# A sparse attention and mixture-of-experts kernel: half a batch more of loads requested ahead of each gate, with a longer FFN lag, a token in place of a drain, and a smaller, later gate

## The chip, the cores and the metric

The kernel runs on one core of one Trainium2 chip. The metric is the device time of one execution in microseconds (us). The engines are PE (matmul; PEld is its weight load), DVE (vector), ACT (scalar), POOL (which here, after some setup, only issues loads) and SP (which issues stores). Each run carries a label, fast or slow. For one core, slow only means over 1.5% above the fastest run of the same kernel.

## The reference, cut to what matters

```python
def _attn_ref(q, k, v):                       # B, H, S, D = 8, 8, 576, 64
    scores = (1 / np.sqrt(D)) * np.matmul(q, k.transpose(0, 1, 3, 2))
    # heads 0-3: the 32 newest positions; heads 4-7: every 4th of the 128 newest
    scores = np.where(masks[None], scores, -1e9)
    ...                                       # softmax
    return np.matmul(attn, v)

def _moe_ref(x, w_gate, w1, w2):              # x: (8, 576, 512); 8 experts, F = 1024
    logits = x.mean(axis=1) @ w_gate          # ONE expert for a whole batch row
    e_idx = np.argmax(logits, axis=1)
    ...                                       # gate_w: softmax weight of that expert
    out[b] = gate_w[b] * (np.maximum(x[b] @ w1[e], 0.0) @ w2[e])
```

Which expert's weights (2 MB of bf16 in SBUF) a batch needs is known only when its attention is finished. So these loads cannot be requested early. The loads of q, k and v could be.

Of the kernel before, what the change touches and what calls it, by code (L numbers as in the profile page):

```python
# [19 lines left out]
P = 128  # L20
B = 8
# [15 lines left out]
DLO = 1024  # L37
HALF = 288
NSLOT = 4
LAG = 6  # L40


@with_exitstack
def kernel(
# [9 lines left out]
):  # L54
    nc = tc.nc
    PSUM = bass.MemoryType.PSUM

    const = ctx.enter_context(tc.tile_pool(name="const", bufs=1))
    ldp = ctx.enter_context(tc.tile_pool(name="ld", bufs=4))
# [46 lines left out]

    GO = (1, 0)

    load_tiles(0)
    load_qk(0, GO[0])  # L110
    identb = const.tile([P, P], BF16, name="identb")
# [6 lines left out]
    nc.gpsimd.iota(dtt[:], pattern=[[1, 4], [4, 16]], base=0, channel_multiplier=-1)  # L118
    load_qk(0, GO[1])
    load_v(0, GO[1])  # L120
    load_tiles(1)
    load_qk(1, GO[0])
    load_v(1, GO[0])
    load_vt(1)
    load_qk(1, GO[1])
    load_v(1, GO[1])

    ones64 = const.tile([P, DH], BF16, name="ones64")
    nc.vector.memset(ones64[:], 1.0)
    wg_t = const.tile([P, 4, E], F32, name="wg_t")  # L130
    for a in range(2):
        for g in range(2):
# [112 lines left out]
    def av_work(b, n):  # L245
        s = state(b)
        g, h2 = GO[n // 2], n % 2
        nd = psN.tile([P, 3 * 512], F32, name="nd", tag="nd", space=PSUM)
        s["nd"] = nd
        vm, vt, pt = loads[b]["v", g], loads[b]["vt"], s["pt"][n]  # L250

        def mm(a, o, n, lhsT, rhs, start, view=None):
            oo = nd[half(a), o : o + n]
            if view is not None:
                oo = view(oo)
            nc.tensor.matmul(oo, lhsT=lhsT, rhs=rhs, start=start, stop=True, skip_group_check=True)  # L256

        def V(a, e, i):
            return vm[half(e), 2 * a + h2, i, :]
# [4 lines left out]
        def part_a():  # L264
# [28 lines left out]
            if g == 0:  # L293
                for a in range(2):
                    mm(a, DLO + 256, 64, ones64[half(0), :], pt[half(0), a, 4 * QB : NP], False)

        def part_b():
            nc.tensor.drain()
            for i in range(4):
                if g == 0:  # L300
                    for e in range(2):
                        for a in range(2):
                            o = NSO + 64 * i if e == 0 else NLO + 64 * (i + 1)
                            mm(a, o, 32, V(a, e, i), pt[half(e), a, QB * i + 64 : QB * i + 96], False)
                else:
                    for a in range(2):
                        mm(a, NLO + 80 * i, 32, V(a, 0, i), pt[half(0), a, QB * i + 64 : QB * i + 96], False)
            if g == 0:
                for e in range(2):
                    for a in range(2):  # L310
                        o = DSO if e == 0 else DLO + 64
                        mm(
                            a, o, 256, ones64[half(e), :], pc(a, e, 64, 96), False,
                            lambda x: x.rearrange("p (i n) -> p i n", n=64)[:, :, 0:32],
                        )
            else:
                for a in range(2):
                    tl = pt[half(0), a, 4 * QB : NP].rearrange("p (r m) -> p r m", r=4)
                    mm(
                        a, NLO, 320, vt[:, 4 * g + 2 * a + h2, :], tl, False,  # L320
                        lambda x: x.rearrange("p (r n) -> p r n", n=80)[:, :, 64:80],
                    )
                for a in range(2):
                    mm(
                        a, DLO, 320, ones64[half(0), :], pc(a, 0, 64, 96), False,
                        lambda x: x.rearrange("p (r n) -> p r n", n=80)[:, :, 0:32],
                    )
                for a in range(2):
                    tl = pt[half(0), a, 4 * QB : NP].rearrange("p (r m) -> p r m", r=4)
                    mm(  # L330
                        a, DLO, 320, ones64[half(0), :], tl, False,
                        lambda x: x.rearrange("p (r n) -> p r n", n=80)[:, :, 64:80],
                    )

        return part_a, part_b

    def emit_ln(b):
        s = st[b]
# [46 lines left out]
    def emit_gate(b):  # L385
        s = st[b]
        pooled = small.tile([P, 4], F32, name="pooled", tag="pooled")
        nc.vector.tensor_tensor(out=pooled[:], in0=s["pool"][:, 0, :], in1=s["pool"][:, 1, :], op=ALU.add)
        lgt = psM.tile([P, 512], F32, name="lgt", tag="M", space=PSUM)
        lg = lgt[:, 0:E]  # L390
        for c in range(4):
            nc.tensor.matmul(  # L392
                lg, lhsT=pooled[:, c : c + 1].to_broadcast([P, P]), rhs=wg_t[:, c, :], start=(c == 0), stop=(c == 3)
            )
        l_sb = small.tile([P, E], F32, name="l_sb", tag="l_sb")
        nc.vector.tensor_copy(out=l_sb[:], in_=lg)
        mx = small.tile([P, 8], F32, name="mx", tag="mx")
        mi = small.tile([P, 8], U32, name="mi", tag="mi")
        nc.vector.max_with_indices(mx[:], mi[:], l_sb[:])
        s["gate"] = (l_sb, mx)  # L400
        e_val = nc.values_load(mi[0:1, 0:1].bitcast(I32), engines=[ET.Pool], min_val=0, max_val=E - 1)
        w1b = wp.tile([P, 4, F], BF16, name="w1b", tag="w1b")
        w2b = wp.tile([P, 8, DM], BF16, name="w2b", tag="w2b")
        s["w1"], s["w2"] = w1b, w2b
        for a in range(2):
            for g in range(2):
                r0 = 256 * g + 128 * a
                nc.gpsimd.dma_start(  # L408
                    out=w1b[half(a), 2 * g : 2 * g + 2, :],
                    in_=moe_w1[ds(e_val, 1), r0 : r0 + 128, :].rearrange("e (h d) f -> d (e h) f", d=DH),  # L410
                )
        nb = b + 2
        if nb < B:
            load_tiles(nb)
            load_qk(nb, GO[0])
        nc.gpsimd.dma_start(out=w2b[:], in_=moe_w2[ds(e_val, 1)].rearrange("e (c p) f -> p (e c) f", p=P))
        if nb < B:
            load_v(nb, GO[0])
            load_vt(nb)
            load_qk(nb, GO[1])  # L420
            load_v(nb, GO[1])

    def emit_gate_w(b):
        s = st[b]
        l_sb, mx = s["gate"]
        negm = small.tile([P, 1], F32, name="negm", tag="negm")
        nc.vector.tensor_scalar_mul(out=negm[:], in0=mx[:, 0:1], scalar1=-1.0 / S)
        esum = small.tile([P, 1], F32, name="esum", tag="esum")
        etmp = small.tile([P, E], F32, name="etmp", tag="etmp")
        nc.scalar.activation(  # L430
            out=etmp[:], in_=l_sb[:], func=AF.Exp, scale=1.0 / S, bias=negm[:], accum_out=esum[:]
        )
        nc.vector.tensor_scalar_add(out=esum[:], in0=esum[:], scalar1=1e-9)
        gbc = small.tile([P, 1], F32, name="gbc", tag="gbc")
        nc.vector.reciprocal(out=gbc[:], in_=esum[:])  # L435
        s["gbc"] = gbc


    def ffn1(b, fc, hf, eng):
# [12 lines left out]
        else:  # L452
            nc.vector.tensor_scalar_max(out=o, in0=hm[:], scalar1=0.0)  # L453

    def ffn2(b, r, eng):
        s = st[b]
        om = psM.tile([P, DM], F32, name="om", tag="M", space=PSUM)
# [6 lines left out]
            nc.scalar.activation(out=osb[:], in_=om[:], func=AF.Copy, scale=s["gbc"][:])  # L464
        else:
            nc.vector.tensor_scalar_mul(out=osb[:], in0=om[:], scalar1=s["gbc"][:])  # L466
        nc.sync.dma_start(out=out[b, r * P : (r + 1) * P, :], in_=osb[:])

    def ffn_tail(b):
        s = st[b]  # L470
# [11 lines left out]
        osx = osp.tile([P, 256], F32, name="osx", tag="osx")  # L482
        nc.vector.tensor_scalar_mul(out=osx[:], in0=ox[:], scalar1=s["gbc"][:])
        for a in range(2):
            nc.sync.dma_start(out=out[b, 512:S, 256 * a : 256 * a + 256], in_=osx[half(a), :])


    ps0 = psS.tile([P, 2, 512], F32, name="psS", tag="S", space=PSUM)
# [11 lines left out]
    def run_T(t):  # L500
        for b, g, nm in tsched.get(t, []):
            emit_T(b, g, nm, 0, "D")
            emit_T(b, g, nm, 1, "A")

    run_T(-2)
    run_T(-1)
    for t in range(NA + LAG + 1):
        b, n = divmod(t, NSLOT)
        pb, pn = divmod(t - 1, NSLOT)
        fb, fk = divmod(t - LAG, NSLOT)  # L510
        att = t < NA
        prev = 0 <= t - 1 < NA
        run_T(t)
        if prev:
            pa, pbb = av_work(pb, pn)
            pa()
        if att:
            emit_S_mm(b, n)
            emit_exp(b, n)
        items = []  # L520
        if 0 <= fb < B:
            if fk < 2:
                for x in range(4):
                    items.append(lambda x=x: (ffn1(fb, 4 * fk + x, 0, "D"), ffn1(fb, 4 * fk + x, 1, "A")))
            elif fk == 2:
                items += [lambda: ffn2(fb, 0, "A"), lambda: ffn2(fb, 1, "D")]
            else:
                items += [lambda: ffn2(fb, 2, "A"), lambda: ffn2(fb, 3, "D"), lambda: ffn_tail(fb)]
        if prev:
            pbb()  # L530
            emit_ln(pb)
        if att:
            emit_mask(b, n)
        if prev:
            emit_rd(pb)
        k0 = len(items) // 2
        for f in items[:k0]:
            f()
        if prev:
            emit_norm(pb, pn)  # L540
        for f in items[k0:]:
            f()
        if prev and pn == NSLOT - 1:
            emit_gate(pb)
            emit_gate_w(pb)


# [28 lines left out]
```

## The kernel before: the parts that the change and the argument touch

Work is laid out in slots. Slot t runs scores (S), exp and mask for one quarter of a batch, and the product with v, the normalization and the division for the quarter of slot t-1. Batch b has slots 4b to 4b+3. Its k and q must be transposed on PE first: the first group of four heads (k in slot 4b-2, q in 4b-1), then the second group (k in slot 4b, q in 4b+1). The FFN of batch b is spread over four slots from slot 4b+LAG on: two of fc1 (`hm`, needs w1), two of fc2 (`om`, needs w2).

```python
LAG = 6
ldp = tc.tile_pool(name="ld", bufs=4)         # q, k, v: four batches
osp = tc.tile_pool(name="osp", bufs=3)        # output tiles
...
def part_b():                                 # second half of the product with v
    nc.tensor.drain()
    ...
def emit_gate(b):
    ...                                       # pooled sum; logits on 128 partitions
    e_val = nc.values_load(mi[0:1, 0:1].bitcast(I32), engines=[ET.Pool], ...)
    for a in range(2):
        for g in range(2):
            nc.gpsimd.dma_start(out=w1b[...], in_=moe_w1[ds(e_val, 1), ...])
    nb = b + 2
    if nb < B:
        load_tiles(nb)
        load_qk(nb, GO[0])                    # first group of batch b+2
    nc.gpsimd.dma_start(out=w2b[:], in_=moe_w2[ds(e_val, 1)]...)
    if nb < B:
        load_v(nb, GO[0]); load_vt(nb)
        load_qk(nb, GO[1]); load_v(nb, GO[1]) # second group of batch b+2
...
for t in range(NA + LAG + 1):
    run_T(t)                                  # transposes, first thing in a slot
    if prev: pa()                             # product, first half
    if att:  emit_S_mm(b, n); emit_exp(b, n)
    if prev: pbb(); emit_ln(pb)               # product, second half
    ...                                       # mask, half of the FFN, norm, other half
    if prev and pn == NSLOT - 1:
        emit_gate(pb); emit_gate_w(pb)        # gate of batch b: end of slot 4b+4
```

All loads go through POOL's one queue in program order.

The softmax here doesn't subtract the row's maximum and nothing guards it: scores larger than these inputs give would overflow.

## Time and profile before

| | before |
|---|---|
| time, median of 3 | 309.23 us (308.3 to 311.2) |
| PE / DVE / ACT busy | 72% / 43% / 42% |
| chain of waits | PE 44%, DMA 25% (k alone 20%) |
| mean granted PE clock | 0.895 |

No engine is full, so the chain of waits and the table of waits are the views to read. The waits table of the kernel before names who waited for whom; its columns are total us, how often, and the longest:

```profile
PEld L190 <- DMA km<-in_k_dram: 49.6, 8, 10.0
PE tp L190 <- DMA km<-in_k_dram: 47.9, 8, 9.8
...
PE hm L446 <- DMA w1b<-in_moe_w_dram: 11.7, 4, 6.5
...
PE lgt L392 <- DVE pooled L388: 9.7, 8, 2.7
```

PE waited 48 us in 8 pieces for k before a transpose. The same table, asked stretch by stretch, splits them: 8.7 us in two pieces at the start, 9.8 us behind gate 0, and 29.4 us in five steady batches (6.4, 8.0, 5.7, 5.9 and 3.4). The chain that ended last, in order of time (start, duration, what), shows the load of k once per batch; its pieces are about 9 us. Here is one batch of the kernel before:

```profile
144.93 9.13 DMA km<-in_k_dram
154.11 1.06 PE tp L190 x31
156.89 2.49 PE hm L446 x12
...
174.48 1.04 PE lgt L392 x8
179.84 9.14 DMA km<-in_k_dram
189.03 1.06 PE tp L190 x31
```

The gate's logits (174.48) come about 5 us before k is even requested (179.84), and k lands 9 us after that. The stretches of the kernel before give the length of each stretch, the busy us of PE, PEld, DVE, ACT and POOL (with counts) in it, then the granted clock, the DMA share and GB/s:

```profile
180.00:186.00 6.00, 3.13 (x26) 1.58 (x24) 1.91 (x6) 0.69 (x1) 4.46 (x7) 1.00 1.01 155
186.00:192.00 6.00, 2.85 (x90) 2.46 (x91) 0.76 (x1) 1.62 (x3) 2.12 (x3) 0.50 1.12 248
...
204.00:210.00 6.00, 4.93 (x46) 2.73 (x48) 2.29 (x7) 2.83 (x5) 0.00 (x0) 1.00 0.17 66
```

While PE stands (from 183 us), its granted clock falls to 0.50 and is still there when work resumes at 189 us. From 204 us, with the loads done, the DMA engines have little to do (share 0.17, 66 GB/s). That fall agrees with the Trainium skill, "TensorE: Matmul & The Clock Gate", Part 1, which says that a PE which has idled for a window is put on half clock until a busy window has passed.

### The profile page before, as it was taken

What the parts mean: (1) busy time and instruction counts of PE and PEld (TensorE: products, weight loads), DVE (VectorE), ACT (ScalarE), POOL (GpSimd) and SP (SyncE); (2) the same over time, 40 slices, a digit from 0 to 9 for tenths busy, and PEclk for the clock granted to TensorE, in tenths of its full rate; (3) what the DMA queues carried; (4) which work ended last, traced back from release to release, by engine and by line L of the source; (5) the groups of instructions that cost most, each with busy time, mean ns of one, the idle gap of its engine ahead of it and who ended that gap; (6) DMA issues with size and microseconds to landing.
All of it is one profiled execution on the core that took longest, in us unless ns stands there. A gap on an engine that the chain in (4) does not pass through costs nothing.

```text
span 309.2 us, 8991 instructions
## 1 busy us (share of the span) xinstructions
PE 223.7 (72%) x3936; PEld 151.6 (49%) x3936; DVE 131.7 (43%) x366; ACT 130.3 (42%) x225; POOL 80.7 (26%) x128
## 2 busy tenths in 40 slices
PE   1565508989299836999299865987599868981894
PEld 1554506754276514755177534754376535640652
DVE  3645413645155532654156532654255533430231
ACT  2465404654067403654057423654167441620230
POOL 8730272007310262005410083005510120021000
PEclk9999999997689985997879895997989996997699
DMA  7990099916997299914999189945999299029803
GB/s 101 185 177 4 9 169 203 127 71 91 217 206 81 79 180 227 173 38 100 193 215 117 72 131 238 198 56 104 195 220 111 72 174 182 2 75 213 140 36 119
DMA packets 49383, 40.97 MB, mean 133 GB/s; under 512 B 23744, under 2 KB 37056, under 8 KB 49344
## 3 DMA queue, kind: packets, MB, share of 16 engines
q0 software_dynamic: 42880, 30.94, 69.5%
q1 hardware_dynamic: 6464, 9.46, 8.9%
q8 instruction: 31, 0.51, 0.6%
q14 instruction: 8, 0.07, 0.1%
HBM read 61.88 MB, written 9.44 MB: 231 GB/s over the span
## 4 chain that ended last, share of the span: by engine, by line
PE 44%; DMA 25%; DVE 10%; issue 8%; ACT 6%; POOL 3%; POOLq 2%
DMA km<-in_k_dram 20%; PE hm L446 19%; PE om L459 10%; DMA w1b<-in_moe_w_dram 6%; PE nd L256 5%; PE tp L190 5%; DVE xt L373 3%; PE lgt L392 3%; ACT pt L233 3%; PE psS L209 3%; DVE ht L453 2%; DVE osb L466 2%; POOL w1b L408 2%; ACT qk L196 1%; DVE pt L240 1%
## 5 line engine op out<-in xcount | busy, mean ns | idle before, releaser
L446 PE MATMUL hm<-xt,w1b 128*128 128x288 bf16 x512 | 78.7, 314 | 12.4 <-DMA w1b<-in_moe_w_dram 11.7
L446 PEld LDWEIGHTS <-w1b 128*128 128x128 bf16 x512 | 53.3, 107 | 34.9 <-issue 11.2
L459 PE MATMUL om<-w2b,ht 128*128 128x512 bf16 x256 | 62.4, 401 | 0.0
L408 POOL DMA_DIRECT2D w1b<-in_moe_w_dram x32 | 19.1, 606 | 133.1 <-DVE gbc L435 61.8
L196 ACT ACTIVATE qk<-tp 128x576 bf16<-128x576 bf16 x32 | 23.2, 726 | 67.6 <-PE tp L190 67.6
L190 PE MATMUL tp<-ident,km 64*64 64x64 bf16 x576 | 16.3, 219 | 48.8 <-DMA km<-in_k_dram 47.9
L451 ACT ACTIVATE ht<-hm 128x288 bf16<-128x288 f32 x64 | 26.2, 409 | 50.3 <-PE hm L446 50.2
L198 DVE COPY qk<-tp 128x576 bf16<-128x576 bf16 x32 | 24.1, 756 | 45.4 <-PE tp L190 45.4
L453 DVE TENSOR_SCALAR ht<-hm 128x288 bf16<-128x288 f32 x64 | 29.2, 456 | 32.6 <-PE hm L446 31.9
L459 PEld LDWEIGHTS <-ht 128*128 128x128 bf16 x256 | 25.1, 103 | 31.1 <-issue 6.0
L190 PEld LDWEIGHTS <-km 64*64 64x64 bf16 x576 | 14.2, 133 | 52.0 <-DMA km<-in_k_dram 49.6
L373 DVE SCALAR_TENSOR_TENSOR xt<-nd,rd 128x320 bf16<-128x320 f32 x64 | 32.4, 544 | 13.9 <-ACT rd L346 13.9
L100 POOL DMA_DIRECT2D vm<-in_v_dram x32 | 23.9, 755 | 52.6 <-DMA w2b<-in_moe_w_dram 30.8
L240 DVE TENSOR_TENSOR pt<-pt,mk 128x896 bf16<-128x896 bf16 x32 | 20.0, 625 | 35.8 <-ACT pt L233 35.8
L233 ACT ACTIVATE pt<-psS 128x896 bf16<-128x896 f32 x32 | 29.1, 911 | 9.4 <-PE psS L209 8.5
L256 PE MATMUL nd<-pt,vm 64*64 64x64 bf16 (+2 forms) x896 | 25.2, 207 | 8.7 <-DVE xt L373 4.2
L256 PEld LDWEIGHTS <-vm 64*64 64x64 bf16 x896 | 18.2, 120 | 15.0 <-issue 14.0
L256 PE MATMUL nd<-pt,ones 64*64 64x128 bf16 (+3 forms) x288 | 24.1, 279 | 0.0
L346 ACT ACTIVATE rd<-lnd 128x576 f32<-128x576 f32 x32 | 21.8, 683 | 1.0
L466 DVE TENSOR_SCALAR osb<-om,gbc 128x512 f32<-128x512 f32 x16 | 12.0, 750 | 24.0 <-PE om L459 24.0
L340 ACT ACTIVATE lnd<-nd 128x576 f32<-128x576 f32 x32 | 20.8, 648 | 1.2 <-PE nd L256 1.2
L209 PE MATMUL psS<-qk 64*64 64x96 bf16 (+2 forms) x576 | 20.3, 247 | 0.0
(52 smaller groups left out, 183.5 us busy)
## 6 DMA issues: line engine op xcount, KB each, us to landing
w1b<-in_moe_w_dram POOLq DMA_DIRECT2D x32, 256.0 KB, 6.2
w2b<-in_moe_w_dram POOLq DMA_DIRECT2D x8, 1024.0 KB, 15.5
out_dram<-osb SPq DMA_DIRECT2D x32, 256.0 KB, 2.3
km<-in_k_dram POOLq DMA_DIRECT2D x16, 288.0 KB, 9.3
qm<-in_q_dram POOLq DMA_DIRECT2D x16, 288.0 KB, 10.8
vm<-in_v_dram POOLq DMA_DIRECT2D x8, 256.0 KB, 15.9
vm<-in_v_dram POOLq DMA_DIRECT2D x32, 64.0 KB, 11.3
out_dram<-osx SPq DMA_DIRECT2D x16, 64.0 KB, 7.7
```

The source lines that it names most:

```text
L190: nc.tensor.transpose(out=tp[half(a), j, :], in_=t[half(a), RH * jh + j, :], identity=ident2[half(a), :])
L196: nc.scalar.activation(out=o, in_=i, func=AF.Copy)
L198: nc.vector.tensor_copy(out=o, in_=i)
L209: nc.tensor.matmul(ps[half(e), a, o : o + rhs.free_size()], lhsT=lhsT, rhs=rhs, start=True, stop=True, skip_group_check=True)
L233: nc.scalar.activation(out=pt[:], in_=s["ps"][:, :, 0:NP], func=AF.Exp, scale=0.125)
L256: nc.tensor.matmul(oo, lhsT=lhsT, rhs=rhs, start=start, stop=True, skip_group_check=True)
L373: nc.vector.scalar_tensor_tensor(out=o, in0=a0, scalar=1.0, in1=a1, op0=ALU.mult, op1=ALU.mult, accum_out=s["pool"][:, w, c : c + 1],)
L408: nc.gpsimd.dma_start(out=w1b[half(a), 2 * g : 2 * g + 2, :], in_=moe_w1[ds(e_val, 1), r0 : r0 + 128, :].rearrange("e (h d) f -> d (e h) f ...
L446: nc.tensor.matmul(hm[:], lhsT=s["w1"][:, c, fc * P : (fc + 1) * P], rhs=s["xt"][:, c, cols], start=(c == 0), stop=(c == 3))
L451: nc.scalar.activation(out=o, in_=hm[:], func=AF.Relu)
L453: nc.vector.tensor_scalar_max(out=o, in0=hm[:], scalar1=0.0)
L459: nc.tensor.matmul(om[:], lhsT=s["ht"][:, fc, r * P : (r + 1) * P], rhs=s["w2"][:, fc, :], start=(fc == 0), stop=(fc == 7))
```

## The change

The intent: ask for half a batch more ahead of each gate; give the weights two more slots before the FFN wants them; take the PE drain, the wide logits and the wait for them out of PE's way. The core of the diff (stores deferred by a slot, the dependency lines of the fence, the order of the FFN's evictions and the rewritten slot order are cut short):

```diff
-LAG = 6
+LAGS = (6, 7, 8, 8, 8, 8, 8, 8)
@@ load_a(b): tiles, first group's k, q, v, and vt;  load_b(b): second group's k, q, v
@@ av_work
+        def fence():
+            token[0] = nc.sync.nop()           # waits for the first half's matmuls
         def part_b():
-            nc.tensor.drain()
+            first[0] = token[0]                # PE waits for SP's nop
@@ emit_gate
-        lg = lgt[:, 0:E]
+        lg = lgt[0:1, 0:E]                     # logits and gate weight on one partition,
+        ...                                    # broadcast later by a small matmul (emit_gate_bc)
-        nb = b + 2
-        if nb < B:
-            load_tiles(nb)
-            load_qk(nb, GO[0])
+        if b == 0:
+            load_a(2)
         nc.gpsimd.dma_start(out=w2b[:], in_=moe_w2[ds(e_val, 1)]...)
-        if nb < B:
-            load_v(nb, GO[0]) ...
+        load_b(b + 2)
+        load_a(b + 3)
@@ main loop
-        run_T(t)                               # transposes before the product and S
         if prev: pa(); fence()
+        flush()                                # stores of the slot before
         if att: emit_S_mm(b, n); emit_exp(b, n)
+        if items: run_T(t)                     # transposes after S
...
+        if gn == 0 and 1 < gb < B + 1:         # slot 4b+5, between the FFN's halves
+            emit_gate(gb - 1); emit_gate_w(gb - 1)
         if prev: emit_norm(pb, pn)
-        if prev and pn == NSLOT - 1:           # end of slot 4b+4
-            emit_gate(pb); emit_gate_w(pb)
```

After the change, gate b asks for the second group of batch b+2 (wanted in slot 4b+8) and the first group of batch b+3 (wanted in slot 4b+10). It asks half a slot later than before; only gate 0 keeps its old place, at the end of slot 4.

More of the change, by code (lines that the diff above doesn't have):

```diff
@@ L56 @@
     PSUM = bass.MemoryType.PSUM
+    SYNC = mybir.DependencyInfo(mybir.DependencyClass.Sync, mybir.DependencyReason.DATA)
     const = ctx.enter_context(tc.tile_pool(name="const", bufs=1))
@@ L107, with load_a, load_b @@
     GO = (1, 0)
+    def load_a(b):
+        if b < B:
+            load_tiles(b)
+            load_qk(b, GO[0])
+            load_v(b, GO[0])
+            load_vt(b)
+    def load_b(b):
+        if b < B:
+            load_qk(b, GO[1])
+            load_v(b, GO[1])
     load_tiles(0)
@@ L120 @@
     load_v(0, GO[1])
-    load_tiles(1)
-    load_qk(1, GO[0])
-    load_v(1, GO[0])
-    load_vt(1)
-    load_qk(1, GO[1])
-    load_v(1, GO[1])
+    load_a(1)
+    load_b(1)
     ones64 = const.tile([P, DH], BF16, name="ones64")
     nc.vector.memset(ones64[:], 1.0)
+    ones1 = const.tile([1, P], F32, name="ones1")
+    nc.vector.memset(ones1[:], 1.0)
     wg_t = const.tile([P, 4, E], F32, name="wg_t")
@@ L249, in av_work @@
         s["nd"] = nd
+        first, lasts = [None], []
         vm, vt, pt = loads[b]["v", g], loads[b]["vt"], s["pt"][n]
@@ L255, in mm @@
                 oo = view(oo)
-            nc.tensor.matmul(oo, lhsT=lhsT, rhs=rhs, start=start, stop=True, skip_group_check=True)
+            x = nc.tensor.matmul(oo, lhsT=lhsT, rhs=rhs, start=start, stop=True, skip_group_check=True)
+            if first[0] is not None:
+                tc.add_manual_dep(x.ins, first[0].ins.name, SYNC)
+                first[0] = None
+            lasts.append(x)
         def V(a, e, i):
@@ L295, in part_a @@
                     mm(a, DLO + 256, 64, ones64[half(0), :], pt[half(0), a, 4 * QB : NP], False)
+        token = [None]
+        def fence():
+            token[0] = nc.sync.nop()
+            for x in lasts:
+                tc.add_manual_dep(token[0].ins, x.ins.name, SYNC)
         def part_b():
-            nc.tensor.drain()
+            first[0] = token[0]
             for i in range(4):
@@ L333, in part_b @@
                     )
-        return part_a, part_b
+        return part_a, fence, part_b
     def emit_ln(b):
@@ L389, in emit_gate @@
         lgt = psM.tile([P, 512], F32, name="lgt", tag="M", space=PSUM)
-        lg = lgt[:, 0:E]
+        lg = lgt[0:1, 0:E]
         for c in range(4):
-            nc.tensor.matmul(
-                lg, lhsT=pooled[:, c : c + 1].to_broadcast([P, P]), rhs=wg_t[:, c, :], start=(c == 0), stop=(c == 3)
-            )
-        l_sb = small.tile([P, E], F32, name="l_sb", tag="l_sb")
+            nc.tensor.matmul(lg, lhsT=pooled[:, c : c + 1], rhs=wg_t[:, c, :], start=(c == 0), stop=(c == 3))
+        l_sb = small.tile([1, E], F32, name="l_sb", tag="l_sb")
         nc.vector.tensor_copy(out=l_sb[:], in_=lg)
-        mx = small.tile([P, 8], F32, name="mx", tag="mx")
-        mi = small.tile([P, 8], U32, name="mi", tag="mi")
+        mx = small.tile([1, 8], F32, name="mx", tag="mx")
+        mi = small.tile([1, 8], U32, name="mi", tag="mi")
         nc.vector.max_with_indices(mx[:], mi[:], l_sb[:])
@@ L411, in emit_gate @@
                 )
-        nb = b + 2
-        if nb < B:
-            load_tiles(nb)
-            load_qk(nb, GO[0])
+        if b == 0:
+            load_a(2)
         nc.gpsimd.dma_start(out=w2b[:], in_=moe_w2[ds(e_val, 1)].rearrange("e (c p) f -> p (e c) f", p=P))
-        if nb < B:
-            load_v(nb, GO[0])
-            load_vt(nb)
-            load_qk(nb, GO[1])
-            load_v(nb, GO[1])
+        load_b(b + 2)
+        load_a(b + 3)
     def emit_gate_w(b):
@@ L425, in emit_gate_w @@
         l_sb, mx = s["gate"]
-        negm = small.tile([P, 1], F32, name="negm", tag="negm")
+        negm = small.tile([1, 1], F32, name="negm", tag="negm")
         nc.vector.tensor_scalar_mul(out=negm[:], in0=mx[:, 0:1], scalar1=-1.0 / S)
-        esum = small.tile([P, 1], F32, name="esum", tag="esum")
-        etmp = small.tile([P, E], F32, name="etmp", tag="etmp")
+        esum = small.tile([1, 1], F32, name="esum", tag="esum")
+        etmp = small.tile([1, E], F32, name="etmp", tag="etmp")
         nc.scalar.activation(
@@ L433, in emit_gate_w, with emit_gate_bc @@
         nc.vector.tensor_scalar_add(out=esum[:], in0=esum[:], scalar1=1e-9)
+        gw = small.tile([1, 1], F32, name="gw", tag="gw")
+        nc.vector.reciprocal(out=gw[:], in_=esum[:])
+        s["gw"] = gw
+    def emit_gate_bc(b):
+        s = st[b]
+        bct = psM.tile([P, 512], F32, name="bct", tag="M", space=PSUM)
+        nc.tensor.matmul(bct[:, 0:1], lhsT=ones1[:], rhs=s["gw"][:], start=True, stop=True)
         gbc = small.tile([P, 1], F32, name="gbc", tag="gbc")
-        nc.vector.reciprocal(out=gbc[:], in_=esum[:])
+        nc.vector.tensor_copy(out=gbc[:], in_=bct[:, 0:1])
         s["gbc"] = gbc
@@ L453, in ffn1, with flush @@
             nc.vector.tensor_scalar_max(out=o, in0=hm[:], scalar1=0.0)
+    stores = []
+    def flush():
+        for f in stores:
+            f()
+        stores.clear()
     def ffn2(b, r, eng):
@@ L466, in ffn2 @@
             nc.vector.tensor_scalar_mul(out=osb[:], in0=om[:], scalar1=s["gbc"][:])
-        nc.sync.dma_start(out=out[b, r * P : (r + 1) * P, :], in_=osb[:])
+        stores.append(lambda: nc.sync.dma_start(out=out[b, r * P : (r + 1) * P, :], in_=osb[:]))
     def ffn_tail(b):
@@ L484, in ffn_tail @@
         for a in range(2):
-            nc.sync.dma_start(out=out[b, 512:S, 256 * a : 256 * a + 256], in_=osx[half(a), :])
+            stores.append(
+                lambda a=a: nc.sync.dma_start(out=out[b, 512:S, 256 * a : 256 * a + 256], in_=osx[half(a), :])
+            )
     ps0 = psS.tile([P, 2, 512], F32, name="psS", tag="S", space=PSUM)
@@ L503, in run_T @@
             emit_T(b, g, nm, 1, "A")
+    runs = {}
+    for b in range(B):
+        for kk in range(NSLOT):
+            runs[NSLOT * b + kk + LAGS[b]] = (b, kk)
     run_T(-2)
     run_T(-1)
-    for t in range(NA + LAG + 1):
+    for t in range(max(runs) + 1):
         b, n = divmod(t, NSLOT)
         pb, pn = divmod(t - 1, NSLOT)
-        fb, fk = divmod(t - LAG, NSLOT)
+        fb, fk = runs.get(t, (-1, 0))
         att = t < NA
         prev = 0 <= t - 1 < NA
-        run_T(t)
-        if prev:
-            pa, pbb = av_work(pb, pn)
-            pa()
-        if att:
-            emit_S_mm(b, n)
-            emit_exp(b, n)
         items = []
-        if 0 <= fb < B:
+        if fb >= 0:
             if fk < 2:
-                for x in range(4):
-                    items.append(lambda x=x: (ffn1(fb, 4 * fk + x, 0, "D"), ffn1(fb, 4 * fk + x, 1, "A")))
+                for x in range(8):
+                    items.append(lambda x=x: ffn1(fb, 4 * fk + x // 2, x % 2, "D" if x < 4 else "A"))
             elif fk == 2:
@@ L529 @@
         if prev:
+            pa, fence, pbb = av_work(pb, pn)
+            pa()
+            fence()
+        flush()
+        if att:
+            emit_S_mm(b, n)
+            emit_exp(b, n)
+        if items:
+            run_T(t)
+        if prev:
+            if not att and items:
+                items.pop(0)()
             pbb()
@@ L535 @@
             emit_rd(pb)
+        if not items:
+            run_T(t)
         k0 = len(items) // 2
@@ L538 @@
             f()
+        gb, gn = divmod(t - 1, NSLOT)
+        if gn == 0 and 0 < gb < B + 1:
+            if gb > 1:
+                emit_gate(gb - 1)
+                emit_gate_w(gb - 1)
         if prev:
@@ L542 @@
             f()
-        if prev and pn == NSLOT - 1:
-            emit_gate(pb)
-            emit_gate_w(pb)
+        if t == NSLOT:
+            emit_gate(0)
+            emit_gate_w(0)
+        if gn == 1 and 0 < gb < B + 1:
+            emit_gate_bc(gb - 1)
+    flush()
 _INS = ['q', 'k', 'v', 'moe_w_gate', 'moe_w1', 'moe_w2']
```

## The prediction

> **What bounds it now.** No engine: the page gives PE 72% busy, DVE 43%, ACT 42%. The chain of waits is PE 44%, DMA 25%, of which the k load is 20%. The waits table has PE waiting 47.9 us for k (8 waits) and 11.7 for w1. The chain in order of time shows a k stall of 7.9 us at 39 us, one of 8.2 to 10.1 in each of the next five batches, then w1 stalls of 8.6 and 8.7 at 248 and 278 us. Each gate asks for w1, then k of two batches on, barely a slot before the transposes want it. The stretches show the queue busy at about 190 GB/s for 25 us, then nearly idle until the next gate (35 us a batch). After each stall the granted clock is 0.5 for some 4 us; the first fc1 slot takes 5.2 us of matmuls, the next 4.36. That agrees with the Trainium skill, "TensorE: Matmul & The Clock Gate", Part 1 (an idle window halves the clock).
>
> **What the change does.**
> 1. Loads half a batch earlier: the five steady k stalls (46 us) go, unless DMA becomes the limit. The first, behind gate 0, stays.
> 2. Lag 8: w1 has about 17 us and takes about 8. The two late w1 stalls (17 us) hide behind the FFN of batch 6. Price: about 8 us of FFN moves into the tail, two slots without FFN save 1.5 each: +5.
> 3. Fewer cold starts, about 1.5 us on six or seven: -10.
> 4. Gate off the path: pooled sum and logits cost PE about 1.0 us waiting and 1.0 of matmul each time: -9; the broadcast gives back 1 to 2.
> 5. Token for drain: the gap before the product's second half is 0.12 to 0.3 us, 32 times: -3.
> 6. Transposes after S, evictions grouped by engine (fc1 no longer waits behind the 1.1 us normalization): -3.
>
> PE alone: 227 by these terms; built from warm slots of about 6 us, 236.
>
> **The new limit.** A batch moves about 5.05 MB (3.87 loads, 1.18 stores). At 190 to 200 GB/s that is 25 to 26.5 us, against about 24 us of PE work. So batches 2 to 5 should run at the queue's pace; tightest is the second group's k, asked three slots ahead behind 2 MB of weights. I add 7 us to the 236.
>
> **Prediction: 243 us, 8 in 10 between 232 and 257.** Faster by over 2%: 0.97; within 2%: 0.02; slower: 0.01.
>
> **What would show it.** Step 1: one k wait of 7 to 9 us near 38 to 47 us, no regular ones; other PE waits on DMA 5 to 15 us, in batches 3 to 6. Step 2: w1 waits under 4 us in all. Step 3: mean granted clock from 0.895 to 0.95 or above, PE busy from 224 to about 210 us, its share above 82%. Step 4: no PE wait on the pooled sum over 0.5 us. Step 5: waits before the second half under 0.3 us. DMA: near 200 GB/s without empty slices between 50 and 190 us.
>
> **What would make it wrong.** If the queue sustains well over 200 GB/s beside busy engines: 232 to 236. If mixed traffic runs below 185 GB/s, or POOL cannot issue ahead (it already waits for old loads, 31 us behind w2), smaller stalls return: 255 or more. If PE is throttled when dense, +8. If fc1 tiles evicted four in a row by one engine (0.41 to 0.46 us each) lag PE's 0.48 us a tile, slots grow.

## The result, and the profile after

| | before | after |
|---|---|---|
| time, median | 310.22 us (308.3 to 311.37, 4 runs) | 286.24 us (284.16 to 286.6, 4 runs, all fast) |
| PE busy | 223.7 us, 72% | 207.4 us, 73% |
| chain of waits | PE 44%, DMA 25% | PE 42%, DMA 33% |
| mean granted clock | 0.895 | 0.922 |

The ratio is 0.9219 (95%: 0.9148 to 0.929). A ratio is the mean time of one kernel's fast runs over that of the other's of the same rounds, so it is not quite the ratio of the medians. The change is faster by 8%, not by the 22% predicted, and 286 us lies outside the range of 232 to 257. The profile after is of the run with the highest granted clock, 0.922; the other three had 0.909 to 0.915.

The waits table after:

```profile
PEld L201 <- DMA km<-in_k_dram: 38.8, 7, 7.4
PE tp L201 <- DMA km<-in_k_dram: 31.9, 6, 7.2
...
PE hm L470 <- DMA w1b<-in_moe_w_dram: 4.0, 3, 1.7
...
PE lgt L415 <- DVE pooled L411: 3.1, 5, 0.6
```

The waits for w1 and for the pooled sum shrank as intended. The waits for k did not go. The two totals of PE are not quite alike (the wait at the start, 8.7 us before, stands after the change in the line of the weight load alone). Stretch by stretch, 7.1 us of 9.8 are left behind gate 0, and 24.9 us of 29.4 in the five steady batches (0.6, 7.2, 5.1, 5.2 and 6.8). The chain in order of time, one batch:

```profile
132.59 0.91 POOL w2b L435
133.50 15.10 DMA km<-in_k_dram
148.63 1.11 PE tp L201 x33
150.12 6.30 PE hm L470 x32
158.00 2.08 PE hm L470 x16
163.66 1.52 issue
166.43 0.91 POOL w2b L435
167.33 14.53 DMA km<-in_k_dram
```

The chain now runs through POOL: w2 is issued, then k, and k takes 15 us to land. POOL's issues in order of time (start, duration, what) give the time of the gate, which I take as the start of its first w1 request:

```profile
130.19 2.38 POOL L429 DMA_DIRECT2D w1b<-in_moe_w_dram  x4 [10.31 <-DVE esum L449]
132.59 0.92 POOL L435 DMA_DIRECT2D w2b<-in_moe_w_dram  x1
133.50 0.57 POOL L92 DMA_DIRECT2D km<-in_k_dram  x1
...
162.97 1.19 POOL L429 DMA_DIRECT2D w1b<-in_moe_w_dram  x2 [11.16 <-PE hm L470]
```

So k, requested at 133.50, is used at 148.63, which is 18.4 us after the gate's first request, and the next gate follows 14.3 us after that. The stretches of the same batch after:

```profile
144.00:150.00 6.00, 1.37 (x56) 1.30 (x56) 1.18 (x3) 0.70 (x2) 1.29 (x2) 0.83 1.15 244
150.00:156.00 6.00, 6.00 (x32) 4.00 (x31) 3.24 (x10) 2.63 (x6) 0.70 (x1) 0.61 1.52 198
156.00:162.00 6.00, 5.38 (x125) 4.17 (x123) 3.64 (x12) 3.77 (x8) 0.00 (x0) 1.00 0.25 25
```

PE stands from about 144 us, works on a clock of 0.61 afterwards, and from 156 us the queue is nearly empty (25 GB/s). A queue that runs empty in every batch does not limit by its mean rate. How fast it works off what stands before k still counts.

Where the 24.9 us between the two profiled spans came from, by the times of the gates: gate 0 comes 2.7 us earlier (34.3 against 37.0), gate 1 follows it as before (34.4 against 34.5), gates 1 to 6 lie 14.3 us closer together (32.0 us a batch against 34.9), and the stretch from gate 6 to the end is 7.8 us shorter.

### The profile page after: what moved, and what is told of

Its sections match the earlier page's. It is cut to its first block, busy times and chain, and to the rows that moved or that the text cites. A ratio compares the mean times of both kernels' runs of the same rounds, so it can differ in the third digit from the quotient of the medians.

```text
span 284.3 us, 9050 instructions
## 1 busy us (share of the span) xinstructions
PE 207.4 (73%) x3952; PEld 143.0 (50%) x3952; DVE 129.1 (45%) x375; ACT 128.3 (45%) x225; POOL 80.5 (28%) x128
## 3 DMA queue, kind: packets, MB, share of 16 engines
q1 hardware_dynamic: 6464, 9.46, 10.1%
## 4 chain that ended last, share of the span: by engine, by line
PE 42%; DMA 33%; issue 9%; DVE 8%; POOL 3%; ACT 2%; POOLq 2%; DVEq 0%
DMA km<-in_k_dram 30%; PE hm L470 21%; PE om L490 8%; PE nd L268 5%; PE tp L201 4%; DMA out_dram<-osb 3%; PE psS L220 2%; POOL w2b L435 2%; DVE xt L396 1%; ACT pt L244 1%; DVE qk L209 1%; POOLq L422 1%; PE lgt L415 1%; DVE pt L251 1%; DVE ht L477 1%
## 5 line engine op out<-in xcount | busy, mean ns | idle before, releaser
L470 PE MATMUL hm<-xt,w1b 128*128 128x288 bf16 x512 | 77.1, 313 | 7.0 <-DMA w1b<-in_moe_w_dram 4.0
L490 PE MATMUL om<-w2b,ht 128*128 128x512 bf16 x256 | 58.2, 380 | 0.0
L201 PE MATMUL tp<-ident,km 64*64 64x64 bf16 x576 | 16.4, 219 | 37.6 <-DMA km<-in_k_dram 31.9
L475 ACT ACTIVATE ht<-hm 128x288 bf16<-128x288 f32 x64 | 25.1, 407 | 35.2 <-PE hm L470 31.9
L490 PEld LDWEIGHTS <-ht 128*128 128x128 bf16 x256 | 23.8, 98 | 27.2
L396 DVE SCALAR_TENSOR_TENSOR xt<-nd,rd 128x320 bf16<-128x320 f32 x64 | 32.3, 541 | 11.1 <-ACT rd L369 11.1
L268 PE MATMUL nd<-pt,vm 64*64 64x64 bf16 (+2 forms) x896 | 24.6, 204 | 17.2 <-DVE xt L396 12.8
L201 PEld LDWEIGHTS <-km 64*64 64x64 bf16 x576 | 14.7, 132 | 38.8 <-DMA km<-in_k_dram 38.8
L268 PEld LDWEIGHTS <-vm 64*64 64x64 bf16 x896 | 17.4, 117 | 23.4 <-issue 13.5
L268 PE MATMUL nd<-pt,ones 64*64 64x128 bf16 (+3 forms) x288 | 22.2, 265 | 0.0
L220 PE MATMUL psS<-qk 64*64 64x96 bf16 (+2 forms) x576 | 18.2, 237 | 3.0 <-DVE qk L209 2.5
## 6 DMA issues: line engine op xcount, KB each, us to landing
w2b<-in_moe_w_dram POOLq DMA_DIRECT2D x8, 1024.0 KB, 14.7
km<-in_k_dram POOLq DMA_DIRECT2D x16, 288.0 KB, 13.6
vm<-in_v_dram POOLq DMA_DIRECT2D x32, 64.0 KB, 14.3
```

The lines of the kernel that those rows point to most:

```text
L201: nc.tensor.transpose(out=tp[half(a), j, :], in_=t[half(a), RH * jh + j, :], identity=ident2[half(a), :])
L220: nc.tensor.matmul(ps[half(e), a, o : o + rhs.free_size()], lhsT=lhsT, rhs=rhs, start=True, stop=True, skip_group_check=True)
L268: x = nc.tensor.matmul(oo, lhsT=lhsT, rhs=rhs, start=start, stop=True, skip_group_check=True)
L396: nc.vector.scalar_tensor_tensor(out=o, in0=a0, scalar=1.0, in1=a1, op0=ALU.mult, op1=ALU.mult, accum_out=s["pool"][:, w, c : c + 1],)
L470: nc.tensor.matmul(hm[:], lhsT=s["w1"][:, c, fc * P : (fc + 1) * P], rhs=s["xt"][:, c, cols], start=(c == 0), stop=(c == 3))
L475: nc.scalar.activation(out=o, in_=hm[:], func=AF.Relu)
```

## The experiments

Eighteen kernels ran, all correct. Times are medians of all runs; n/m is how many were fast, and the mean is of those.

| kernel | median us | fast mean us | fast |
|---|---|---|---|
| after | 286.24 | 285.8 | 4/4 |
| a1 k before w2 | 259.7 | 255.4 | 1/4 |
| a2 six output buffers | 281.42 | 281.5 | 4/4 |
| a3 drain back | 286.44 | 286.5 | 4/4 |
| a4 loads alone (from before) | 285.83 | 284.6 | 3/4 |
| b1 both groups a batch ahead, six buffers | 247.32 | 247.3 | 4/4 |
| b2 k before w2, six buffers | 252.0 | 252.2 | 4/4 |
| b3 loads, k first, lags (from before) | 258.42 | 256.5 | 2/4 |
| b4 loads, lags (from before) | 271.86 | 271.1 | 3/4 |
| c1 gate at its old place | 255.27 | 255.3 | 4/4 |
| c2 c1 and six buffers | 253.47 | 253.3 | 4/4 |
| c3 lags alone (from before) | 298.15 | 298.0 | 4/5 |
| c4 batch ahead and lags (from before) | 259.88 | 255.6 | 1/4 |
| d1 b1 with the gate at its old place | 239.02 | 239.0 | 4/4 |
| d2 c1, transposes at their old place | 264.83 | 263.8 | 3/4 |
| d3 c1, logits on 128 partitions | 261.66 | 261.9 | 4/4 |
| d4 b4 with the gate late | 296.82 | 296.2 | 4/4 |
| e1 d1 with lag 7 | 245.09 | 245.2 | 4/4 |
| e2 d1 with the drain | 244.08 | 244.3 | 6/6 |

The kernel before gave medians of 310.1 to 311.6 beside them.

Two theories stood at the start. **Order**: k of the second group waits behind 2 MB of weights that cannot be requested before the gate. **Bandwidth**, the one of the prediction: the queue as a whole is full.

### a1: k before w2

```diff
+        if b + 2 < B:
+            load_qk(b + 2, GO[1])
         nc.gpsimd.dma_start(out=w2b[:], ...)
-        load_b(b + 2)
+        if b + 2 < B:
+            load_v(b + 2, GO[1])
         load_a(b + 3)
```

> The changed kernel with one move at each gate: the second group's k and q of two batches on are requested between w1 and w2, not behind w2. Same bytes. Theory 'order' (the five remaining k waits of 5 to 8 us come from k queued behind 2 MB of weights, 18 to 20 us after the gate's first request): k lands about 5 us (1 MB at 200 to 240 GB/s) sooner, the waits of PE on k fall from 32 us to about 10 to 14 (the first one of 7 stays), cold starts after them shrink too: 258 to 270 us against 286. Theory 'bandwidth' (the queue runs at its pace, as predicted before the result): the same bytes take the same time, 282 to 288 us.

Measured: 259.7 us median; only one of four runs counts as fast, 255.4, so there is no interval. Every run (255.4 to 261.9) lies at least 22 us below every run of the change. The waits table of a1 (its profile is of a run marked slow, 259.98 us):

```profile
PEld L201 <- DMA km<-in_k_dram: 14.2, 3, 7.5
PE tp L201 <- DMA km<-in_k_dram: 8.2, 2, 7.4
```

The same bytes in another order, and the PE wait for k falls from 31.9 to 8.2 us; 7.4 us of that is the wait behind gate 0, which the prediction had left standing. In the steady batches 0.8 us is left of 24.9. Bandwidth falls as the reason; order stands.

### a2: six output buffers

```diff
-    osp = ctx.enter_context(tc.tile_pool(name="osp", bufs=3))
+    osp = ctx.enter_context(tc.tile_pool(name="osp", bufs=6))
```

> The changed kernel with six buffers instead of three for the output tiles, so that evictions need not wait for the stores that are now issued a slot later. Theory 'late stores cost the tail': the waits of DVE before osb on stores (5.8 us in the last batch, 4.5 us one batch before) go, 279 to 283 us against 286. Theory 'order': between the k waits nothing is gained, as any time won before a k wait is waited out there; at most 3 us in the tail: 283 to 286 us.

Measured: 281.42 us, ratio 0.9075 (0.9018 to 0.9131), 4 us better than the change and as the first theory said: the waits of DVE for a store, 9.6 us in two pieces in the change, are gone. But the name "late stores" turned out half wrong, see b3.

### a3: the drain back

```diff
         def part_b():
-            first[0] = token[0]
+            nc.tensor.drain()
```

> The changed kernel with the PE drain in place of the token over SP (same place in PE's order, after the S matmuls and the transposes). Theory 'the token gains': 0.12 to 0.3 us in up to 32 places, 286 to 289 us. Rival 'the token costs' (it queues on SP behind the stores of the slot before[...]): the drain is faster, 280 to 284 us. If the k waits swallow both, 285 to 287.

Measured: 286.44 us, no difference. The small waits of PE before this code are fewer with the token (13.5 us in 20 with it, 19.4 us in 48 with the drain); the k waits swallow them. e2 below repeats this where nothing does.

### a4: the load schedule alone, on the kernel before

The edit is the emit_gate part of the diff above, in the kernel before.

> The kernel before with only the load schedule of the change (half a batch more ahead, w2 before the second group); lag 6, drain, gate and transposes as before. Theory 'the loads are the gain': the first group's k wait (9 us, five times) goes, w1 now shows instead at lag 6 (about 3 us, six times), the second group's k, 18 to 20 us after the gate, is just in time for three full slots: 272 to 284 us against 310. Rival 'the lag is needed': w1 waits take most of it back, 290 to 300 us.

Measured: 285.83 us median, fast mean 284.6 (3 of 4), just above the first expectation. Its PE waits are for w1 now (18.5 us in 11, against 11.7 in 4 before). The load schedule by itself gives all that the whole change gives. So the lag and the small parts together are worth nothing in the change: either each is worth nothing there, or one costs what the other gains.

### b4: loads and lags, none of the small parts; c3: the lags alone

```diff
-LAG = 6
+LAGS = (6, 7, 8, 8, 8, 8, 8, 8)
-        fb, fk = divmod(t - LAG, NSLOT)
+        fb, fk = runs.get(t, (-1, 0))
```

> The kernel before with the change's load schedule and lags, none of the small parts. a4 (lag 6) took 285.8 and waited for w1 before each batch's fc1; the whole change takes 286.2 and waits for k. Theory 'the lag only turned the w1 wait into the k wait': 280 to 287 us, with k waits of 4 to 7 us in five batches in place of w1 waits. Theory 'lag gains and the small parts lose it': 270 to 277 us.

> The kernel before with the change's lags only; loads as before. The prediction gave the lag minus 17 us (two late w1 waits hidden behind the FFN of batch 6) plus 5 (more FFN in the tail), and the 9 us k waits stay: 295 to 302 us against 310. If the lag only moves waits, 306 to 312.

Measured: b4 271.86 us, c3 298.15 us. The lag is a true gain: 13 us alone (298.0 against 311.1 fast means) and 13.5 us on top of the loads (284.6 to 271.1). My first theory for b4, that the lag only turns one wait into another, fell by its time. The exchange itself took place: from a4 to b4, PE's waits for w1 fall from 18.5 us to 1.1 and those for k rise from 11.7 to 32.3. Of the 10.2 us between the two profiled spans, 6.7 lie after gate 6, where the last waits for w1 were. And since b4 is 14.7 us faster than the whole change, the small parts lose about that much in it.

### c1: the gate at its old place; c2: and six output buffers

```diff
-        if gn == 0 and 0 < gb < B + 1:
-            if gb > 1:
-                emit_gate(gb - 1); emit_gate_w(gb - 1)
...
-        if t == NSLOT:
-            emit_gate(0); emit_gate_w(0)
+        if prev and pn == NSLOT - 1:
+            emit_gate(pb); emit_gate_w(pb)
```

> The changed kernel with the gate back at the end of the slot that follows the batch's last attention slot, where the kernel before has it (logits still on one partition); everything else as changed. b4 has lags and loads but none of the small parts and takes 271.9 against 286.2 of the whole change, so a small part costs 14 us. Theory 'the gate was moved half a slot later, and it is the start of the path gate to weights to k': each of five k waits shrinks by about 3 us: 268 to 275 us. Rival 'the cost lies in other small parts (late stores, transposes after S)': 283 to 288 us.

> c1 and six output buffers. If gate place and output buffers explain the whole 14 us (a2 won 5), this is at or below b4: 264 to 271 us. If something else in the small parts costs time, it stays above 274.

Measured: c1 255.27 us, c2 253.47 us. Half a slot of delay of the gate had cost 30 us, twice what I expected. The waits of PE for k (7.5 us of them behind gate 0) and for the pooled sum in c1:

```profile
PE tp L201 <- DMA km<-in_k_dram: 14.3, 5, 7.5
...
PE lgt L415 <- DVE pooled L411: 1.0, 1, 1.0
```

The chain of c1 in a window shows one batch:

```profile
125.70 14.11 DMA km<-in_k_dram
...
139.85 0.69 PE tp L201 x32
...
140.79 4.03 PE hm L470 x32
144.82 0.28 PE lgt L415 x8
```

and POOL's issues in order of time:

```profile
122.39 2.36 POOL L429 DMA_DIRECT2D w1b<-in_moe_w_dram  x4 [6.45 <-DVE gw L451]
...
147.04 1.19 POOL L429 DMA_DIRECT2D w1b<-in_moe_w_dram  x2 [4.35 <-PE nd L268]
```

This gives the mechanism. It is a loop: a gate requests weights and k; k lets the transposes of slot 4b+8 run; in PE's order, the next gate comes after that slot. The loop for gate 3 of five kernels, from such lines:

| kernel | gate to transposes of that k | transposes to next gate | loop |
|---|---|---|---|
| before | 11.5 | 23.4 | 34.9 |
| after | 18.4 | 14.3 | 32.8 |
| d4: b4, gate late | 19.4 | 14.9 | 34.3 |
| b4: loads and lags | 18.3 | 10.3 | 28.6 |
| c1: after, gate at its old place | 17.5 | 7.2 | 24.7 |

(In the kernel before it is the first group's k, used in slot 4b+6; in the others the second group's, in slot 4b+8.) In the last column stands the time of this one turn. Over all the turns from gate 1 to gate 6 the means are, in the same order, 34.9, 32.0, 33.2, 28.9 and 26.2 us. As a measure of what PE needs for a batch: the gates of d1 below, in which k is not waited for after gate 0, are 23.0 to 24.5 us apart.

The change shortened the second part and lengthened the first. In the change and in c1 alike, the rest of the slot that waited for k lies in the loop, but in the change it runs on a cold clock (its 32 fc1 matmuls take 6.30 us against 4.03 in c1). Moving the gate from the end of slot 4b+4 into slot 4b+5 adds the next slot's product, S and transposes and half of its FFN: in all 7.1 us between the change and c1, not the 3 us of half a warm slot. The means give 5.8 us a turn, over five turns 29 of the 30 us. In c1 the turn has come down to near what PE needs for a batch, so the steady waits for k are 6.8 us in all instead of 24.9, and PE is busy for 199.0 us instead of 207.4, at a higher clock (0.963 against 0.922). The waits and the cold restarts together make the gain so large.

### d4: the gate late in b4; d1: the gate at its old place where k is off the loop

d4 makes the c1 edit in reverse in b4. d1 is b1 (below) with the c1 edit.

> b4 (loads and lags of the change, none of the small parts, 271.9 us) with only the gate moved half a slot later, to where the change has it. Loop theory: k to next gate grows from 10.3 us by 2.5 to 4 us in five batches: 284 to 292 us. If the gate's place matters only together with the other small parts: 270 to 275.

> b1 (both groups a batch ahead, six output buffers, 247.3 us) with the gate back at its old place. Loop theory: k is not in the loop here, so the gate's place matters only for the one w1 wait of batch 1 (9.4 us in b1's chain): 243 to 248 us. Rival 'an early gate is better in itself (less in PE's way, loads spread better)': 230 to 240 us.

Measured: d4 296.82 us, so 25 us lost with the gate's place alone (271.1 to 296.2), more than I expected and in the direction of the loop. The gate and its k in d4, from POOL's issues and the chain:

```profile
136.69 2.36 POOL L420 DMA_DIRECT2D w1b<-in_moe_w_dram  x4 [12.38 <-DVE esum L440]
...
171.04 1.19 POOL L420 DMA_DIRECT2D w1b<-in_moe_w_dram  x2 [11.94 <-PE hm L453]
```

```profile
140.00 16.08 DMA km<-in_k_dram
...
156.12 1.06 PE tp L202 x18
```

d1 239.02 us against 247.32 of b1: 8 us where I expected at most 4, far from the 30 us of c1, and inside the range of the rival, that an early gate is better in itself. The remainder is not k. The chain of b1 has two waits for w1 which d1's does not show, at batch 1 and at the last batch:

```profile
71.72 9.43 DMA w1b<-in_moe_w_dram
...
218.51 8.13 DMA w1b<-in_moe_w_dram
```

A late gate delays w1 as well. But that is the smaller part: these pieces are whole loads, and PE itself waited for w1 only 4.3 us in b1. By the gates, 4.8 us of the gain lie in the middle, between gates 2 and 6 (24.5 us a batch in b1, 23.3 in d1). There PE of b1 waits 2.5 us for the pooled sum and 4.3 us for DVE's normalization, against none and 1.6 in d1. So in this order of PE the late gate is in PE's way, as the rival had it; which of these waits make up the 8 us was not tested.

### b1 and b2: both groups a whole batch ahead, or k before w2, with six output buffers

```diff
         nc.gpsimd.dma_start(out=w2b[:], ...)
-        load_b(b + 2)
-        load_a(b + 3)
+        if b == 0:
+            load_b(2)
+        load_a(b + 3)
+        load_b(b + 3)
```

> The changed kernel with both groups of a batch requested three batches on (at gate 0 also the second group of batch 2), behind w2, and six output buffers. Nothing of k is then wanted within 20 us of its request after the first. Theory 'order': the k waits after the first are gone entirely (a1 kept one of 11 us in the chain, in batch 2), and the tail wait on stores too: 246 to 253 us, against 259.7 of a1 and 281.4 of a2. Theory 'bandwidth': a1 already sits at the queue's pace, so only the stores' share is won: 254 to 258.

> The changed kernel with the second group's k and q ahead of w2 (as a1) and six output buffers (as a2). a2 won about 5 us where the k waits stood; a1's chain still holds two waits of 7 us on a store (157 and 230 us). If these are real losses: 248 to 255 us; if they only hide another wait, 256 to 259.

Measured: b1 247.32 us, b2 252.0 us, both within the first expectation. With both groups a batch ahead, PE's wait for k is 12.7 us in two pieces, one at the very start and one behind gate 0, which still has to ask for batch 2's second group. Of bandwidth, the stretches of d1 (which moves the same bytes) say the most; their GB/s count stores too:

```profile
119.00:142.00 23.00, 22.65 (x491) 15.80 (x488) 15.32 (x44) 15.45 (x29) 10.43 (x16) 1.00 1.28 223
142.00:165.00 23.00, 22.83 (x501) 16.04 (x498) 15.38 (x44) 15.59 (x29) 9.03 (x15) 1.00 1.27 222
```

PE is busy 22.65 of 23 us on a full clock while loads and stores together move 223 GB/s. The prediction had taken 190 to 200 GB/s as the ceiling; that it was read from stretches in which the queue was not always full is my guess, and was not tested.

### b3 and c4: the small parts where k is not in the way

b3 is the kernel before with the loads of a1 and the lags; c4 is the kernel before with the loads of b1 and the lags.

> The kernel before with the load schedule of a1 (k and q ahead of w2) and the change's lags; drain, gate on 128 partitions at its old place, transposes and stores as before. This is a1 without all the small parts. If the small parts (gate off the path, token, transposes moved) are worth the 12 us that the prediction counted: 268 to 273 us against 259.7. If they are worth nothing, as a3 and a4 hint, 257 to 262; if the late stores made them a loss, 250 to 256.

> The kernel before with the loads of b1 (both groups three batches on, behind w2) and the change's lags, drain, old gate, old transposes, three output buffers. Against b1 (247.3): the small parts where no k wait swallows or magnifies them. If they are worth the 12 us of the prediction: 256 to 262 us. If they are worth little and three buffers cost 5: 250 to 255.

Measured: b3 258.42 us (fast mean 256.5, 2 of 4), level with a1 (255.4, one fast run). c4 259.88 us (one fast run, 255.6). With so few fast runs both are weak. b3 taught something else. It issues its stores at once, as before, and yet its chain has the same waits for a store:

```profile
158.07 7.44 DMA out_dram<-osb
...
228.56 7.13 DMA out_dram<-osb
```

A 256 KB store took a median of 2.3 us from issue to landing in the kernel before, 6.5 us in b3 and 6.7 us in the change. So the deferral is not needed for these waits; it is three buffers with stores that take three times as long beside a busy queue. The Trainium skill, "DMA: Bandwidth & Descriptors", section "Queues, rings and completion order", says that each DMA engine takes turns between the queues that have work, packet by packet; these landings agree with it, though no run here isolates it.

### d2 and d3: transposes and logits, undone in c1

```diff
d2: +        run_T(t)                  # back to the start of the slot
d3: -        lg = lgt[0:1, 0:E]
    +        lg = lgt[:, 0:E]          # and the gate weight on 128 partitions, no broadcast
```

> c1 (gate at its old place, 255.3 us) with the transposes back at the start of the slot. Loop theory: the first half of the product and S now come after k's arrival, not before it, so that k to next gate grows from 7.2 us by 1 to 2 us in the batches that wait: 258 to 265 us. If the place of the transposes is worth nothing: 254 to 257.

> c1 with the logits and the gate weight on 128 partitions, without the broadcast matmul. The eight matmuls of the logits took 1.04 us in b4 and 0.28 to 0.36 in c1; with the old form the loop grows by about 0.7 us a batch and PE loses 0.7 us eight times, less the broadcast: 256 to 262 us. If worth nothing: 254 to 256.

Measured: d2 264.83 us (fast mean 263.8), d3 261.66 us (261.9): the transposes' place is worth 8.5 us and the narrow logits 6.6 us in c1. Both lie in the second part of the loop, and both are expected by it. Their sum, 15.1 us, is near the 15.8 us between b4 and c1; that they add up was not tested.

### e1 and e2: the lag and the token in the fastest kernel

e1 has `LAGS = (6, 7, 7, 7, 7, 7, 7, 7)`; e2 has the a3 edit.

> d1 with lag 7 instead of 8 from batch 2 on: about 4 us less FFN stands alone after the last attention slot, but w1 has two slots (about 12 us) from gate to first use, where it lands 6 to 9 us after requests that the busy queue spreads over 3 to 4 us. If w1 still comes in time: 234 to 238 us against 239.0. If w1 shows as a wait in most batches: 240 to 246.

> d1 with the PE drain in place of the token. The prediction counted the token at 3 us (0.1 us in 32 places). If so: 241 to 243 us against 239.0. If the drain's wait is hidden behind weights already loading, or the token costs as much: 238 to 240.

Measured: e1 245.09 us, so lag 7 loses 6 us. Its chain has an 8.7 us load of w1 before the last batch's FFN, which d1 has not, but PE waits for w1 only 3.8 us, and there alone, not in most batches as the second expectation had it. By the gates, 5.0 us of the 7.8 between the two profiled spans lie between gates 1 and 6 (24.5 us a batch against 23.5); what makes them was not found. e2 244.08 us (6 runs, 243.59 to 245.27), above both expectations: where no wait swallows it, the token is worth 5.3 us. The waits tables of e2, then of d1, for the weight loads of the product:

```profile
PEld L268 <- issue: 13.3, 40, 2.0
```

```profile
PEld L268 <- issue: 6.4, 8, 2.4
```

With the drain there are 40 such small waits, with the token 8; the difference is 6.9 us.

## Why the prediction was wrong, point by point

- **The bound of the kernel before** was read rightly in kind: a wait for k once a batch, and cold clocks after it. Its size was not. The 46 us of step 1 add up the loads of k in the chain (8.2 to 10.1 us each); PE itself waited 29.4 us in these five batches.
- **Step 1, "the five steady k stalls (46 us) go, unless DMA becomes the limit", failed.** Five steady k waits stayed, now for the second group: 24.9 us of PE waiting instead of 29.4. The prediction named this k "tightest", but only as part of a bandwidth limit worth 7 us. Its own figures, 2 MB of weights and 288 KB of k at 190 GB/s, make about 12 us from the gate, against three slots of 6 us, so no wait was expected. Measured: 18.4 us from the gate to the transposes, 3.3 us of them POOL's issues ahead of k (the stretches add up to about 3.4 MB moved in these 18.4 us, 1 MB more than the weights and k, and SP issues six stores, 1.18 MB, from 136.8 us on; so stores and other loads are the likely rest, which no run isolates); and PE stood from about 144 us, some 14 us after the gate, not 18, which fits a gate that has moved half a slot later. What was not seen at all is that this is a loop, so that a few us in it set the time of every batch. a1 (0.8 us of steady k waits left) and b1 (none) show the order, c1 and d4 the loop.
- **"The new limit", the queue at 190 to 200 GB/s, was wrong.** a1 moves the same bytes in the same queue 26 to 30 us faster, and d1 runs at 223 GB/s with PE full.
- **Step 2, the lag, was right in mechanism and size**: -17 and +5 make -12; c3 measured -13, and the waits of PE for w1 (11.7 us before) are gone in c3 and 4.0 us in the change. The split is a little off: the step put -9 at the end and -3 into two slots without FFN; of the 10.1 us between the two profiled spans 5.1 lie after gate 6 and 4.7 between gates 1 and 6.
- **Step 3, fewer cold starts**: PE busy fell to 207 us as predicted (210), but the clock reached 0.922, not 0.95, and PE's share 73%, not 82%, since five long waits remained. d1 has 0.975 and 83%.
- **Step 4, the gate off PE's path, "-9", had the wrong sign.** Narrow logits gain (6.6 us in c1). The gate's later place, which was meant to save PE a wait of 1 us each time, costs 30 us in the change (c1) and 25 in the old form (d4), since all that PE does between the landed k and the next gate is part of the loop. And there was nothing to save: in the new slot order with the gate at its old place PE waits 1.0 us in all for the pooled sum (c1, d3), with the late gate 3.1 us. With the gate's place alone undone the kernel takes 255.3 us, so here, where k is in the loop, this one sign makes 30 of the 43 us between 243 predicted and 286 measured.
- **Step 5, the token, "-3"**: 0 in the change (a3), 5.3 in d1 (e2). Right mechanism, invisible where a later wait swallows it.
- **Step 6, "-3"**: the transposes alone are worth 8.5 us in c1 (d2), because they stand in the loop; the grouped evictions were not isolated.
- **The figure for PE alone, 227 to 236, was nearly reached** by d1, 239 us, in which the steady waits are gone.

Still open: the exact split of d1's last 8 us against b1, the 5 us in the middle of e1, what lengthens k's way beside the weights, and the order of evictions. Fast runs of a1, b3 and c4 are too few for intervals.

## What to carry to other kernels

Look for the loop: a result that decides a load, the load, the work it lets run, and the next such result in the same engine's order. While it is longer than the work of the busiest engine for one turn, its length is the time of a turn, so anything placed between a landed load and the next request costs its full time, and anything requested behind the undecidable loads waits for them; ask for what does not depend on the decision a whole turn earlier, and put the decision as early as its data allows. Gains of small parts (a drain, narrow logits) can measure as nothing until such a wait is gone, so try them again afterwards: the version with both groups a batch ahead, the gate at its old place and six output buffers runs in 239.0 us, a ratio of 0.7684 (0.764 to 0.7728) to the kernel before.

## What the Trainium skill lacked or had wrong

- "DMA: Bandwidth & Descriptors", section "Anatomy of one DMA", gives about 2.0 us plus bytes over 436 GB/s for one load from POOL's queue; for k's 288 KB, as written, that is an estimate of 2.7 us. The quickest k load of the change took 4.3 us, the median 13.6 and the longest 16.8, and a1 shows that what stands before k in the queue makes much of it. A kernel needs the queue's sum, and the page gives no rule for it beside stores and engines at work; d1 moved 223 GB/s with PE 98% busy.
- "Perfetto Trace Analysis", section "Optimization Strategy", says that consistent bubbles can mean too few buffers. Here the bubble of every batch was a late request (with the same buffers a1 took all but 0.8 us of the steady k waits away, c1 all but 6.8 of 24.9); buffers were the smaller part (4 us, a2). The page has nothing on loops between a load and the next request.
- "TensorE: Matmul & The Clock Gate", Part 1, agrees with these traces: a granted clock of 0.50 at the end of a 6 us wait of PE for k before, and 0.61 over the 6 us after the wait in the change.
- No page gives what a PE drain within a kernel costs against a wait on another engine's no-op: 5.3 us for 32 of them (e2 against d1).
